# The left rows of four batches as one pair of tiles in the seven-product scheme

## The chip, the cores and the metric

The kernel runs on one core of one Trainium2 chip. The metric is the device time of one execution in microseconds (us). Five engines matter: PE multiplies matrices, DVE (VectorE) and ACT (ScalarE) do elementwise work, SP issues most transfers, and 16 DMA engines carry them. Each engine works through its own queue in order and waits at its head for semaphores. Matrix products land in PSUM, of which this kernel uses four banks for output sums (tag `acc`), two for the hidden layer (tag `h`) and two for other products (`bg`).

## The reference

```python
def _attn_ref(q, k, v, phi):                     # 8 batches, 8 heads, 576 rows, width 64, 32 memories
    a = softmax(phi over its rows)
    k_m = np.einsum('bhsm,bhsd->bhmd', a, k)
    v_m = np.einsum('bhsm,bhsd->bhmd', a, v)
    attn = softmax(scale * q @ k_m.T)
    return attn @ v_m

x = attn_out as 4608 x 512
h = x @ w_in                                     # 512 x 2048
g = h * sigmoid(h)
return g @ w_out                                 # 2048 x 512
```

## The kernel before

A batch has 576 rows: 512 main rows, which are four tiles of 128, and 64 left rows. Two batches' left rows make one tile of 128, kept in `gleft` (128 partitions, 16 chunks of the hidden width, 2 x 64 rows). Operands of the products are split into a high and a low part in a 32-bit format that PE takes at full rate, and each product is three matmuls: high x high, high x low, low x high.

Per batch, attention is folded into the first layer: `p_mm` multiplies the batch's memory with `w_in` (its result, split in two by ACT L647 and DVE L649, is the tile `pm`), and the hidden layer is attention weights (`aparts`) times `pm`. `s_back` turns the weights of the next batch into place (two transposes on DVE, L461, into a tile `aT`; a copy on ACT, L462) and `s_low` makes their low part (DVE L467).

Batches 0 and 1 work in 16 steps: `ffn1` (12 matmuls, 288 columns), `silu` (ACT L694, L696), `split`, and `ffn2` into four `acc` tiles, one per main row tile (12 matmuls of 512 columns). At the end of a batch `store` copies the four `acc` tiles on ACT (L724) and sends them out. The tiles of the first two copies share one buffer (`cva`), which the fourth copy takes again, so it waits until the first two have been sent.

Batches 2 to 7 use a scheme of seven products for a pair of row tiles and a pair of chunks, in place of eight. A batch has two pairs of tiles (t = 0, 1) and eight pairs of chunks (j): 16 steps. In each, `ffn1s` makes the hidden layer of the step (12 matmuls into `h`, one buffer), `forms` applies silu (ACT L825 into the buffer `gbuf`, L827 for the left rows), builds sums and differences (DVE L830, L833, L834), and splits them (ACT L829, L839; DVE L840, L841) into two alternating sets of buffers in `aparts` and `gparts`. `st_step` then does 7 x 3 = 21 matmuls of 256 columns into four `sum` banks. After j = 7 `st_out` copies banks 0 and 1 (ACT L884), adds (DVE L891, four adds, and three later in `rest`) and stores. PE runs `ffn1s` of step s + 1 ahead of `st_step` of step s.

Behind batches 1, 3, 5 and 7 comes a left phase of four steps for the one tile of left rows of two batches. Behind batch 1 it is plain: `left_step`, 48 matmuls of 512 columns into `accleft`, with `t1_load` fetching changed weight blocks into `wo_hi` and `wo_lo` after each step. Behind the others `left_st` does 96 matmuls of 256 columns (eight products' worth, three banks `lsum`). The operands are made by `left_split` (ACT L916, DVE L917). The left phase is also where `s_back` and `s_low` for the next even batch run (slot `NFC + 3`), with `aT` in `gbuf`, which the left phase does not use otherwise.

What sets the order: the code is written step by step; the table of events (`ev(batch, slot, function)`) says what else runs in which slot (`run`). PE and ACT follow the written order, DVE and SP are placed by a scheduler within the constraints. All transfers named `L88` go through SP's one queue in the order of issue.

## Time and profile before

| what | value |
|---|---|
| median of 3 runs | 692.94 us (692.68 to 693.82) |
| profiled execution, first to last instruction | 692.1 us |
| DVE busy | 515.7 us (75%) |
| ACT busy | 367.7 us (53%) |
| transfers | 93.93 MB, 136 GB/s mean |
| left phase behind batch 1 | from about 194.5 us |
| left phase behind batch 3, 5, 7 | from about 358.6, 521.9, 677.1 us |

A row of a timeline or of the chain gives the start in us, the duration in us, the engine, the line and operation, out<-in with shapes, a count where equal rows are merged, and in brackets the idle time before it with what ended it. A row of windows gives, per stretch, busy time and count of each engine, the granted clock of PE as a share of full speed, the share of DMA engines busy, and GB/s.

### The profile page before, as it was taken

How to read it: one execution, taken by the hardware profiler on the slowest of the kernel's cores; microseconds unless marked ns; L12 is line 12 of the kernel's file. 1: busy time of each engine (PE TensorE's matmuls, PEld its weight loads, DVE VectorE, ACT ScalarE, POOL GpSimd, SP SyncE). 2: the span in 40 equal slices, each digit the busy share in tenths (PEclk: the TensorE clock that was granted, in tenths of full speed). 3: DMA queues.
4: the chain of work that ended last, by engine and by line, in shares of the span. 5: the costliest groups of instructions: out<-in, count | busy, mean ns of one | idle time of the engine just before them, and what ended most of it. 6: DMA issues, size and time to landing. Idle time of an engine off the chain costs nothing.

```text
span 692.1 us, 14815 instructions
## 1 busy us (share of the span) xinstructions
PE 674.7 (97%) x5932; PEld 596.3 (86%) x5932; DVE 515.7 (75%) x1084; ACT 367.7 (53%) x676; POOL 0.7 (0%) x6
## 2 busy tenths in 40 slices
PE   8999999999999999999999999999999999999997
PEld 3578777887788988899998999898989989889997
DVE  3897899788938678877875668786875667776753
ACT  3788684532624545654644545564554645654441
POOL 0000000000000000000000000000000000000000
PEclk9999999999999999999999999999999999999999
DMA  9898983234261463243430335224422203210001
GB/s 342 311 336 282 310 322 129 121 108 152 76 232 25 131 212 114 77 148 123 177 117 16 117 131 166 106 93 153 172 85 79 77 2 131 90 71 17 31 1 46
DMA packets 38228, 93.93 MB, mean 136 GB/s; under 512 B 4752, under 2 KB 22032, under 8 KB 34576
## 3 DMA queue, kind: packets, MB, share of 16 engines
q1 hardware_dynamic: 37136, 90.22, 37.7%
q10 hardware_dynamic: 1024, 2.77, 1.0%
q8 instruction: 47, 0.77, 0.5%
q14 instruction: 21, 0.17, 0.1%
HBM read 77.22 MB, written 15.73 MB: 134 GB/s over the span
## 4 chain that ended last, share of the span: by engine, by line
PE 76%; DVE 6%; ACT 2%; issue 1%; DMA 1%; SPq 0%; DVEq 0%; ACTq 0%
PE sum L850 32%; PE h L811 20%; PE acc L710 7%; PE lsum L850 5%; PE h L669 4%; PE bg L631 4%; PE accleft L710 2%; PE bg L333 1%; ACT gbuf L825 1%; PE bg L380 1%; DMA fm<-fm 1%; DVE pm L649 1%; DVE gbuf L830 0%; DVE sc L428 0%; DVE smx L424 0%
## 5 line engine op out<-in xcount | busy, mean ns | idle before, releaser
L811 PE MATMUL h<-aparts,pm 128*128 128x288 f32 x1152 | 168.8, 295 | 0.1
L811 PEld LDWEIGHTS h<-aparts,pm 128*128 128x128 f32 x1152 | 157.0, 188 | 0.7 <-ACT gleft L827 0.4
L825 ACT ACTIVATE gbuf<-h 128x512 f32<-128x512 f32 x96 | 57.2, 596 | 128.7 <-PE h L811 126.7
L850 PE MATMUL sum<-wo_hi,aparts 128*128 128x256 f32 x384 | 103.9, 293 | 0.0
L830 DVE TENSOR_TENSOR gbuf<-gbuf 128x256 f32<-128x256 f32 x96 | 40.6, 423 | 81.8 <-ACT gbuf L825 81.1
L850 PE MATMUL sum<-kept,aparts 128*128 128x256 f32 x576 | 100.1, 282 | 0.0
L850 PE MATMUL sum<-wo_lo,aparts 128*128 128x256 f32 x384 | 100.0, 282 | 0.0
L850 PEld LDWEIGHTS sum<-wo_hi,aparts 128*128 128x128 f32 x384 | 72.7, 189 | 20.6 <-ACT gleft L827 16.7
L839 ACT ACTIVATE aparts<-gbuf 128x512 fp32r<-128x512 f32 x86 | 54.4, 633 | 64.0 <-DVE gbuf L834 64.0
L710 PE MATMUL acc<-wo_hi,gparts 128*128 128x512 f32 x256 | 86.3, 396 | 0.2
L850 PEld LDWEIGHTS sum<-kept,aparts 128*128 128x128 f32 x576 | 82.5, 191 | 0.0
L841 DVE TENSOR_TENSOR gparts<-gbuf,aparts 128x512 fp32r<-128x512 f32 x86 | 59.6, 693 | 18.8 <-ACT aparts L839 18.4
L850 PE MATMUL sum<-wo_hi,gparts 128*128 128x256 f32 x384 | 73.2, 281 | 0.0
L850 PEld LDWEIGHTS sum<-wo_lo,aparts 128*128 128x128 f32 x384 | 73.1, 190 | 0.0
L850 PE MATMUL sum<-kept,gparts 128*128 128x256 f32 x288 | 65.5, 282 | 0.0
L710 PEld LDWEIGHTS acc<-wo_hi,gparts 128*128 128x128 f32 x256 | 47.8, 188 | 14.5 <-issue 2.6
L850 PEld LDWEIGHTS sum<-wo_hi,gparts 128*128 128x128 f32 x384 | 59.4, 190 | 0.0
L669 PEld LDWEIGHTS h<-aparts,pm 128*128 128x128 f32 x372 | 51.8, 188 | 7.7 <-issue 2.7
L669 PE MATMUL h<-aparts,pm 128*128 128x288 f32 x372 | 56.2, 299 | 1.3 <-DVE aparts L467 1.0
L710 PE MATMUL acc<-wo_lo,gparts 128*128 128x512 f32 x128 | 50.4, 394 | 0.8 <-DVE wo_lo L182 0.7
L829 ACT ACTIVATE aparts<-gbuf 128x384 fp32r<-128x384 f32 x96 | 50.4, 525 | 0.0
L850 PEld LDWEIGHTS sum<-kept,gparts 128*128 128x128 f32 x288 | 47.9, 190 | 0.0
(206 smaller groups left out, 989.9 us busy)
## 6 DMA issues: line engine op xcount, KB each, us to landing
win<-win_saved SPq DMA_DIRECT2D x24, 1024.0 KB, 4.9
kv<-in_kv SPq DMA_DIRECT2D x28, 516.0 KB, 4.8
q<-in_q SPq DMA_DIRECT2D x16, 576.0 KB, 4.9
raw<-in_w_in SPq DMA_DIRECT2D x14, 512.0 KB, 7.5
raw<-in_w_out SPq DMA_DIRECT2D x6, 1024.0 KB, 5.8
win_saved<-win SPq DMA_DIRECT2D x4, 1024.0 KB, 8.8
phi<-in_phi SPq DMA_DIRECT2D x7, 576.0 KB, 6.3
out<-oo SPq DMA_DIRECT2D x26, 128.0 KB, 1.8
```

The source lines that it names most:

```text
L333: nc.tensor.matmul(pt[p][M * r : M * (r + 1), :KVW], e[:, p, c, M * r : M * (r + 1)], kvt[c][:, p, r], start=c == 0, stop=False, skip_grou ...
L380: nc.tensor.matmul(to[M * r : M * (r + 1)], kvT[D * p : D * (p + 1), 0, r], at[b]["q", hf][D * p : D * (p + 1), r, f : f + n], start=True, ...
L631: nc.tensor.matmul(bg[M * r : M * (r + 1), p, :w].rearrange("p (k f) -> p k f", f=P), kvT[D * p : D * (p + 1), 1, r], src[D * p : D * (p + ...
L669: nc.tensor.matmul(h[:, hf, :HALF], wt[:, p, fs], a[:, p, hf * HALF : (hf + 1) * HALF], start=n[hf] == 0, stop=n[hf] == 5, skip_group_chec ...
L710: nc.tensor.matmul(acc[key], gt[:, cs], wt[:, fc], start=fc == 0 and n == 0, stop=fc == NFC - 1 and n == 2)
L811: nc.tensor.matmul(h[:, i, :HALF], wt[:, p, f : f + P], a[:, p], start=n == 0, stop=n == 5)
L825: nc.scalar.activation(gbuf[:, :MAIN].rearrange("p (i f) -> p i f", i=2), h[:, :, :w], AF.Silu)
L829: nc.scalar.activation(hi[:, :3], g[:, 1:4], AF.Copy)
L830: nc.vector.tensor_tensor(g[:, 4:6], g[:, :1].broadcast_to([P, 2, P]), g[:, 1:3], op=ALU.subtract)
L839: nc.scalar.activation(hi[:, 3:], g[:, 4:], AF.Copy)
L841: last_split.append(nc.vector.tensor_tensor(lo[:, 3:], g[:, 4:], hi[:, 3:], op=ALU.subtract))
L850: nc.tensor.matmul(sums[bank][:, place * Q : (place + 1) * Q], gt[:, k], wt, start=bank not in begun, stop=True, skip_group_check=True,)
```

## The change

The left rows of batches 0 to 3 become one pair of tiles (t = `LEFTS`) of the seven-product scheme behind batch 3, and those of batches 4 to 7 behind batch 7. There is no left phase behind batches 1 and 5 any more. The activations of the first two batches of each four are saved to DRAM (`left_save`, 1 MB in four pieces) and fetched back, 128 KB a step, into two buffers that are the unused ends of `aparts` (`left_load`). `left_forms` builds the operands of a step from the fetched tile and `gleft`: three activations on ACT, four subtractions and three splits on DVE. A left phase has eight steps of 21 matmuls. `t1_load` moves from the left phase into the slots of batch 1. `s_back` and `s_low` always run in slot 14; for even batches `aT` is still in `gbuf`. The last matmuls of batch 1 are run behind `ffn1s` of batch 2's first step, ahead of that step's `forms`. Rows of a pair of left tiles lie in two pieces of 64 in the output, so each store is two transfers.

```diff
-    def left_step(b, n, gs):
...
+    LEFTS, WITH_LEFTS = 2, (3, 7)
...
-    def t1_load(n):
-        for j in (2 * n, 2 * n + 1):
-            for w, q in ((wo_hi, 0), (wo_lo, Q)):
-                load(as_f32(w[:, 2 * j, Q:]), saved[j][:, q : q + Q])
+    def t1_load(j):
+        for w, q in ((wo_hi, 0), (wo_lo, Q)):
+            load(as_f32(w[:, 2 * j, Q:]), saved[j][:, q : q + Q])
...
+        if t == LEFTS:
+            one, two = ([(c * S + MAIN, LEFT) for c in (a, a + 1)] for a in (b - 1, b - 3))
+        else:
+            r = b * S + 2 * t * P
+            one, two = [(r + P, P)], [(r, P)]
...
-        ev(*((b, 9) if t == 0 else (b, NFC + 1) if b % 2 else (b + 1, 3)), rest)
-
-    def left_split(b, n):
...
-    def left_st(b, n, gs):
...
+        if t == LEFTS and b == B - 1:
+            rest()
+        else:
+            ev(*((b, 9) if t == 0 else (b, NFC + 1) if t == 1 and b in WITH_LEFTS else (b + 1, 3)), rest)
+
+    left_saved = hbm.tile([P, NFC, 2 * LEFT], F32, name="left_saved")
+    left_home = [aparts[:, k, 1, TF:] for k in range(2)]
+    left_in = {}
+
+    def left_save(fcs):
+        load(left_saved[:, fcs], gleft[:, fcs])
+
+    def left_load(j):
+        load(as_f32(left_home[j % 2]), left_saved[:, 2 * j : 2 * j + 2].rearrange("p i f -> p (i f)"))
+        left_in[j] = as_f32(left_home[j % 2]).rearrange("p (i f) -> p i f", f=P)
+
+    def left_forms(j):
+
+        g = form_src
+        hi, lo = form_high[j % 2], form_low[j % 2]
+        two, one = left_in.pop(j), gleft[:, 2 * j : 2 * j + 2]
+        nc.scalar.activation(hi[:, 0:3:2], one, AF.Copy)
+        nc.scalar.activation(hi[:, 1], two[:, 1], AF.Copy)
+        nc.vector.tensor_tensor(g[:, 5], two[:, 0], two[:, 1], op=ALU.subtract)
+        nc.vector.tensor_tensor(g[:, 6], one[:, 0], g[:, 5], op=ALU.subtract)
+        nc.vector.tensor_tensor(g[:, 4], two[:, 0], one[:, 0], op=ALU.subtract)
+        s4 = nc.vector.tensor_tensor(g[:, 7], one[:, 1], g[:, 6], op=ALU.subtract)
+        nc.scalar.activation(hi[:, 3:], g[:, 4:], AF.Copy)
+        behind(nc.vector.tensor_tensor(lo[:, 0:3:2], one, hi[:, 0:3:2], op=ALU.subtract).ins, s4)
+        behind(nc.vector.tensor_tensor(lo[:, 1], two[:, 1], hi[:, 1], op=ALU.subtract).ins, s4)
+        last_split.append(nc.vector.tensor_tensor(lo[:, 3:], g[:, 4:], hi[:, 3:], op=ALU.subtract))
+        return hi, lo
...
-        turn = NFC + 3 if b % 2 else 14
+        turn = 14
...
+    for k in range(3):
+        ev(5, 10 + 2 * k, left_save, slice(4 * k, 4 * k + 4))
+    ev(6, 0, left_save, slice(12, NFC))
+    for b in WITH_LEFTS:
+        for j in range(NP):
+            ev(b, 15 if j < 2 else NFC + j - 1, left_load, j)
...
+                ev(*((b, max(2 * j + 2, int(1.5 * j + 3.5))) if j < NP - 1 else (b + 1, 0)), t1_load, j)
+            for k in range(3):
+                ev(b, 4 * k + 4, left_save, slice(4 * k, 4 * k + 4))
+            ev(b + 1, 0, left_save, slice(12, NFC))
...
             h = ffn1s(b, t, j)
+            if prev[0] == "main":
+                finish(range(NI))
+                prev = None
             part = forms(b, t, j, h)
...
-        if b % 2:
-            for n in range(NLS):
-                gs = left_split(b, n)
-                if b > 1:
-                    run(b, NFC + n)
-                finish((0, 1, 2, 3))
-                prev = ("left", b, n, gs)
+        if b in WITH_LEFTS:
+            for j in range(NP):
+                part = left_forms(j)
+                run(b, NFC + j)
+                finish(range(NI))
+                prev = ("st", b, LEFTS, j, part)
```

First place, the end of batch 1. This is PE before, from the last matmuls of the last main tile (`acc3`):

```order
L710 MATMUL acc3_1248<-wo_hi_76,gparts_79 128x512
L710 MATMUL acc3_1248<-wo_lo_77,gparts_79 128x512
L710 MATMUL acc3_1248<-wo_hi_76,gparts_79 128x512
L710 MATMUL accleft_1984<-wo_hi_76,gparts_79 128x512
L710 MATMUL accleft_1984<-wo_lo_77,gparts_79 128x512
L710 MATMUL accleft_1984<-wo_hi_76,gparts_79 128x512 x2
```

And PE after, from the same matmuls, which now stand behind the first `ffn1s` of batch 2; `h_2025` is the second `ffn1s` of batch 2, and `bg` is a `p_mm`:

```order
L709 MATMUL acc3_1249<-wo_hi_76,gparts_79 128x512
L709 MATMUL acc3_1249<-wo_lo_77,gparts_79 128x512
L709 MATMUL acc3_1249<-wo_hi_76,gparts_79 128x512
L803 MATMUL h_2025<-aparts_81,pm_1835 128x288 x12
L630 MATMUL bg_2047<-win2_2_1824,kvT2_1661 32x512 x8
L842 MATMUL sum0_2065<-wo_hi_76,aparts_81 128x256
```

ACT after, at the same place: the four stores of batch 1 (L723), and behind them the silu of batch 2's first step (L817 reads `h_1975`, L819 its left rows); this order is as before:

```order
L723 ACTIVATE oo_1991<-acc0_1237 128x512
L723 ACTIVATE oo_1991<-acc1_1241 128x512
L723 ACTIVATE o_2002<-acc2_1245 128x512
L723 ACTIVATE oo_2008<-acc3_1249 128x512
L817 ACTIVATE gbuf_82<-h_1975 128x512
L819 ACTIVATE gleft_80<-h_1975 128x2x32
```

Between the last `acc3` matmul and the second `ffn1s`, PE had the 48 matmuls of `accleft` and now has nothing; the second `ffn1s` needs the `h` buffer that L819 reads last.

Second place, ACT at the end of batch 3. Before, from the silu of its last step (`h_3850`); L916 is `left_split`, L884 the copies of banks 0 and 1, L462 the copy of `s_back`:

```order
L825 ACTIVATE gbuf_82<-h_3850 128x512
L827 ACTIVATE gleft_80<-h_3850 128x2x32
L829 ACTIVATE aparts_81<-gbuf_82 128x384
L839 ACTIVATE aparts_81<-gbuf_82 128x512
L916 ACTIVATE aparts_81<-gleft_80 128x512
L884 ACTIVATE oo_3916<-sum0_3556 128x512
L884 ACTIVATE oo_3916<-sum1_3557 128x512
L916 ACTIVATE gparts_79<-gleft_80 128x512 x2
L916 ACTIVATE aparts_81<-gleft_80 128x512
L462 ACTIVATE aparts_81<-gbuf_82 128x2x288
```

And after, where L461 is the copy of `s_back`, L817 to L831 the last step of the batch, L931, L932 and L937 the activations of `left_forms`, and L876 the copies of banks 0 and 1:

```order
L461 ACTIVATE aparts_81<-gbuf_82 128x2x288
L817 ACTIVATE gbuf_82<-h_3799 128x512
L819 ACTIVATE gleft_80<-h_3799 128x2x32
L821 ACTIVATE aparts_81<-gbuf_82 128x384
L831 ACTIVATE aparts_81<-gbuf_82 128x512
L931 ACTIVATE aparts_81<-gleft_80 128x2x128
L932 ACTIVATE aparts_81<-aparts_81 128x128
L937 ACTIVATE aparts_81<-gbuf_82 128x512
L876 ACTIVATE oo_3875<-sum0_3501 128x512
L876 ACTIVATE oo_3875<-sum1_3502 128x512
```

The copy of `s_back` has moved from behind the copies of the banks to ahead of the batch's last silu, and ahead of the copies of the banks stands L937, which waits for DVE's four subtractions.

Third place, DVE at the same time after the change, from the first step of `left_forms` (L933 to L940 are its lines; L894 is an add of `st_out`):

```order
L936 TENSOR_TENSOR gbuf_82<-gleft_80,gbuf_82 128x128
L938 TENSOR_TENSOR gparts_79<-gleft_80,aparts_81 128x2x128
L939 TENSOR_TENSOR gparts_79<-aparts_81 128x128
L940 TENSOR_TENSOR gparts_79<-gbuf_82,aparts_81 128x512
L894 TENSOR_TENSOR x_3876<-sum2_3503,oo_3875 128x256
L933 TENSOR_TENSOR gbuf_82<-aparts_81 128x128
L894 TENSOR_TENSOR x_3876<-sum2_3503,x_3876 128x256
L894 TENSOR_TENSOR oo_3875<-oo_3875 128x256
L934 TENSOR_TENSOR gbuf_82<-gleft_80,gbuf_82 128x128
L894 TENSOR_TENSOR oo_3875<-x_3876,sum3_3504 128x256
```

And before, from the only split that stood ahead of the adds (L917 is `left_split`, L891 an add of `st_out`):

```order
L917 TENSOR_TENSOR aparts_81<-gleft_80,aparts_81 128x512
L891 TENSOR_TENSOR x_3917<-sum2_3558,oo_3916 128x256
L891 TENSOR_TENSOR x_3917<-sum2_3558,x_3917 128x256
L891 TENSOR_TENSOR oo_3916<-oo_3916 128x256
L917 TENSOR_TENSOR gparts_79<-gleft_80,gparts_79 128x512
L891 TENSOR_TENSOR oo_3916<-x_3917,sum3_3559 128x256
```

The four adds that empty banks 2 and 3 now stand behind seven operations of `left_forms`, not one split, and two more of them stand between the adds. In the program after, the first step of the left pair takes the banks as they come free: its first product waits for the copy of bank 0, its third for the copy of bank 1, its fourth for the second add, its sixth for the fourth add.

More of the change, by code (lines that the diff above doesn't have):

```diff
@@ L33 @@
 NI = MAIN // P
-NLS = 4
 FULLC = S // P
@@ L734, in main_step @@
                 store((b, i), [(b * S + i * P, P)])
-    def left_step(b, n, gs):
-        for i in range(NI):
-            ffn2(gs, slice(i * P, (i + 1) * P), n * NI + i, (b, "left"))
-        if n == NLS - 1:
-            store((b, "left"), [((b - 1) * S + MAIN, LEFT), (b * S + MAIN, LEFT)], b == B - 1)
     Q = DMODEL // 2
@@ L886, in st_out, with put @@
         c12, c22 = x[:, 0], x[:, 1]
-        r = b * S + 2 * t * P
-        one, two = slice(r + P, r + 2 * P), slice(r, r + P)
+        if t == LEFTS:
[3 more added lines that the diff above has]
+            one, two = [(r + P, P)], [(r, P)]
+        def put(rows, cs, x):
+            at_ = 0
+            for k, (r, n) in enumerate(rows):
+                (nc.scalar if k and b == B - 1 else nc.sync).dma_start(out[r : r + n, cs], x[at_ : at_ + n])
+                at_ += n
+        left, right = slice(0, Q), slice(Q, DMODEL)
         def add(to, a, c, op=ALU.add):
@@ L896, in st_out @@
         add(c21, c22, sums[3][:, :Q], ALU.subtract)
-        nc.sync.dma_start(out[one, :Q], c11)
-        nc.sync.dma_start(out[two, :Q], c21)
+        put(one, left, c11)
+        put(two, left, c21)
         def rest():
@@ L903, in rest @@
             add(c12, c12, p3)
-            nc.sync.dma_start(out[two, Q:], c22)
-            nc.sync.dma_start(out[one, Q:], c12)
-        ev(*((b, 9) if t == 0 else (b, NFC + 1) if b % 2 else (b + 1, 3)), rest)
-    def left_split(b, n):
-        flat = gparts.rearrange("p k n f -> p (k n f)")
-        home = (aparts[:, 0, 1], flat, flat[:, 2 * MAIN :], aparts[:, 1, 1])[n]
-        g = gleft[:, n * NI : (n + 1) * NI].rearrange("p c f -> p (c f)")
-        gs = home[:, :MAIN], home[:, MAIN : 2 * MAIN]
-        if b == 1:
-            return split(g, gs=gs if n == 3 else None)
-        nc.scalar.activation(gs[0], g, AF.Copy)
-        last_split.append(nc.vector.tensor_tensor(gs[1], g, gs[0], op=ALU.subtract))
-        return gs
@@ L920, in left_st @@
-    def left_st(b, n, gs):
-        if n == 0:
-            sums[:] = [ps.tile([P, DMODEL], F32, tag="acc", name=f"lsum{i}", bufs=NI) for i in range(3)]
-            begun.clear()
-        part = [x.rearrange("p (n f) -> p n f", f=P) for x in gs]
-        last = n == NLS - 1
-        if last:
-            o = sb.tile([P, DMODEL], F32, tag="cva", name="ol", bufs=1)
-            x = sb.tile([P, Q], F32, tag="cva1", name="xl", bufs=1)
-        for bank, (ks, q) in enumerate((((0,), 0), ((1,), 0), ((0, 1), 1))):
-            cs = slice(q * Q, (q + 1) * Q)
-            for i in range(2):
-                for k in ks:
-                    fc = 2 * (2 * n + i) + k
-                    product(bank, 0, part, 2 * i + k, (wo_hi[:, fc, cs], wo_lo[:, fc, cs]), HIGH + LOW)
-            if not last:
-                continue
-            if bank == 0:
-                nc.scalar.activation(x, sums[0][:, :Q], AF.Copy)
-                continue
-            nc.vector.tensor_tensor(o[:, cs], sums[bank][:, :Q], x, op=ALU.add)
-            for k, r in enumerate((b - 1, b)):
-                queue = nc.scalar if b == B - 1 and k else nc.sync
-                queue.dma_start(out[r * S + MAIN : r * S + S, cs], o[k * LEFT : (k + 1) * LEFT, cs])
@@ new lines, in rest @@
+            put(two, right, c22)
+            put(one, right, c12)
+        if t == LEFTS and b == B - 1:
[10 more added lines that the diff above has]
+        left_in[j] = as_f32(left_home[j % 2]).rearrange("p (i f) -> p i f", f=P)
@@ L1178, in finish @@
             main_step(prev[1], prev[2], prev[3], tiles)
-        elif prev[0] == "left" and tiles[0] == 0:
-            if prev[1] < 2:
-                left_step(prev[1], prev[2], prev[3])
-                t1_load(prev[2])
-            else:
-                left_st(prev[1], prev[2], prev[3])
         elif prev[0] == "st" and tiles[0] == 0:
```

## The prediction

> **What bounds the kernel now.** I read the busy shares first, then the waits of PE, then the chain of work that ended last, and last the timelines at the places that the change touches.
>
> ```profile
> PE 674.7 (97%) x5932; PEld 596.3 (86%) x5932; DVE 515.7 (75%) x1084; ACT 367.7 (53%) x676; POOL 0.7 (0%) x6
> PE 76%; DVE 6%; ACT 2%; issue 1%; DMA 1%; SPq 0%; DVEq 0%; ACTq 0%
> PE h L380 <- ACT gleft L827: 4.7, 5, 1.3
> ```
>
> PE works for 674.7 of the span's 692.1 us, the chain runs mostly over PE, and PE's dearest wait is 4.7 us in five pieces of at most 1.3. So PE is the bound: a matmul less is worth its time, and any new hole in PE costs its length. DVE (75%) and ACT have slack on the average, not at each place.
>
> **1. Work taken off PE: 5.3 us.** The chain, one row per run of matmuls (start, duration, count):
>
> ```profile
> 194.47 8.17 PE accleft L710 x36
> 204.23 2.76 PE accleft L710 x12
> 326.58 2.49 PE sum L850 x21
> 677.08 11.52 PE lsum L850 x96
> ```
>
> Batch 1's left phase is 8.17 + 2.76 = 10.93. Behind batch 7 96 matmuls take 11.52, or 0.120 each; the phases behind 3 and 5 have the same 96, and I count them alike. Together 10.93 + 3 x 11.52 = 45.5 before. After, 16 steps of 21 matmuls of the same width: 16 x 2.49 to 16 x 2.52 (21 x 0.120), 39.8 to 40.3. The saving is 5.2 to 5.7; I take 5.3.
>
> **2. A hole between batches 1 and 2: +3.3.** (Rows: chain, ACT, the transfers of 180 to 212 us with count, KB each and median us to landing, and a window with PE, PEld, DVE, ACT and POOL, the clock, the DMA share, GB/s.)
>
> ```profile
> 189.01 5.46 PE acc L710 x24
> 202.64 1.59 PE h L811 x12
> 192.53 1.22 ACT L724 ACTIVATE oo<-acc 128x512 f32<-128x512 f32 x2 [2.71 <-PE acc L710]
> 196.05 0.60 ACT L724 ACTIVATE oo<-acc 128x512 f32<-128x512 f32 x1 [1.62 <-DMA out<-oo]
> 204.26 0.60 ACT L825 ACTIVATE gbuf<-h 128x512 f32<-128x512 f32 x1 [7.61 <-PE h L811]
> 204.76 0.22 ACT L827 ACTIVATE gleft<-h 128x64 f32<-128x64 f32 x1
> out<-oo SPq DMA_DIRECT2D x3, 256.0 KB, 2.2
> 190.00:192.00 2.00, 2.00 (x10) 1.68 (x9) 2.00 (x5) 0.00 (x0) 0.00 (x0) 1.00 0.79 270
> ```
>
> Before, the fourth store copy waits on ACT until the first two are out: the second ends at 193.75, the fourth starts at 196.05, 2.30 later. PE has 8.17 us of `accleft` meanwhile. After, PE runs step 14 of batch 1 (half of 5.46, to 191.74), the first `ffn1s` of batch 2 (1.59, to 193.33), step 15 (2.73, to 196.06), and then wants the second `ffn1s`. Its `h` buffer is read by the silu, and that stands on ACT behind the four stores. Step 15 completes a tile each 0.68 us, at 194.0, 194.7, 195.4 and 196.1; the second copy ends some 0.6 behind its tile, at 195.35; the fourth copy starts 2.30 later, at 197.65. Then 0.50 to the silu's start, 0.50 to the left silu (204.26 to 204.76), 0.22 for it and 0.04 to hand over: 198.9 against 196.06, a hole of **2.85**. Behind the waiting copy stand also batch 2's splits, which come later still but inside what PE then has to do. On SP's queue 768 KB more fall here (the last weight blocks of `t1_load`, the last save, the first left loads); at 270 GB/s that is 2.9 us, part of it ahead of a store, so the hole lies between 1.3 (if no store is waited for: the fourth copy at its tile's end, 196.1, and then the same 0.50 + 0.50 + 0.26) and 2.85 + 1.65 = 4.5. I take 3.3, near the computed end.
>
> **3. `s_back` ahead of batch 3's last silu: +1.2.**
>
> ```profile
> 351.95 1.23 DVE L649 TENSOR_TENSOR pm<-bg,pm 128x1024 fp32r<-128x1024 f32 x1 [0.22 <-ACT pm L647]
> 363.02 0.83 DVE L461 STREAM_TRANSPOSE gbuf<-sc 128x288 f32<-128x288 f32 x2
> 364.61 0.76 DVE L467 TENSOR_TENSOR aparts<-gbuf,aparts 128x576 fp32r<-128x576 f32 x1 [0.75 <-ACT aparts L462]
> 353.64 0.60 ACT L825 ACTIVATE gbuf<-h 128x512 f32<-128x512 f32 x1 [1.72 <-PE h L811]
> 354.27 0.53 ACT L829 ACTIVATE aparts<-gbuf 128x384 fp32r<-128x384 f32 x1
> 355.38 0.63 ACT L839 ACTIVATE aparts<-gbuf 128x512 fp32r<-128x512 f32 x1 [0.59 <-DVE gbuf L834]
> 355.96 0.28 PE L850 MATMUL sum<-wo_hi,aparts 128*128 128x256 f32 x1
> ```
>
> `s_back` and `s_low` take 363.02 to 365.37, 2.35 us, and hold `gbuf`, which the silu needs. In slot 14 they start behind L649 (353.18 less an overlap of 0.09) and free `gbuf` at 353.09 + 2.35 = 355.44, so the silu starts at 355.48, not 353.64: 1.84 late. Its first high parts are ready at 354.80 + 1.84 = 356.64, and PE wants them at 355.96: 0.68. Six matmuls later (0.72) it wants the parts of L839, ready at 356.01 + 1.84 = 357.85, and stands at 357.36: 0.5 more. Together 1.2. Behind batch 5 there is no L649 ahead of it in that slot; the same reckoning leaves +0.3. If DVE gets to the transposes early, both are nothing.
>
> **4. The banks' hand-over at a left phase: +1.2 behind batch 7, +1.9 behind batch 3.**
>
> ```profile
> 673.17 0.29 DVE L833 TENSOR_TENSOR gbuf<-gbuf 128x128 f32<-128x128 f32 x1
> 673.50 0.29 DVE L834 TENSOR_TENSOR gbuf<-gbuf 128x128 f32<-128x128 f32 x1
> 673.71 0.55 DVE L840 TENSOR_TENSOR gparts<-gbuf,aparts 128x384 fp32r<-128x384 f32 x1
> 674.49 0.69 DVE L841 TENSOR_TENSOR gparts<-gbuf,aparts 128x512 fp32r<-128x512 f32 x1 [0.23 <-ACT aparts L839]
> 675.10 0.69 DVE L917 TENSOR_TENSOR aparts<-gleft,aparts 128x512 fp32r<-128x512 f32 x1
> 676.04 0.60 ACT L884 ACTIVATE oo<-sum 128x512 f32<-128x512 f32 x1 [1.06 <-PE sum L850]
> 676.88 0.60 ACT L884 ACTIVATE oo<-sum 128x512 f32<-128x512 f32 x1 [0.24 <-PE sum L850]
> 676.92 0.28 PE L850 MATMUL lsum<-wo_hi,aparts 128*128 128x256 f32 x1
> 677.17 0.42 DVE L891 TENSOR_TENSOR x<-sum,oo 128x256 f32<-128x256 f32 x1 [1.39 <-ACT oo L884]
> ```
>
> An operation of this size starts 0.33 behind one it depends on and 0.21 behind one it doesn't (673.17, 673.50, 673.71). After, DVE begins the four subtractions at 675.10, L936 ends at 676.14, L937 runs from 676.18 to 676.81, and the copy of bank 0, behind it on ACT, starts at 676.72 in place of 676.04, to 677.32. PE's first product starts at 677.36, not 676.92: 0.44. DVE's splits and the first adds follow, with L933 and L934 of the next step between them; the second add ends at 678.43, and the fourth product waits for it 0.38; the fourth add ends at 679.32, and the sixth product waits 0.41. Sum 1.2. Behind batch 3 the 1.84 of part 3 comes on DVE too: 1.07 in place of 0.44, sum 1.9.
>
> **5. The end: +2.3.**
>
> ```profile
> 688.31 0.28 PE L850 MATMUL lsum<-wo_hi,aparts 128*128 128x256 f32 x1
> 688.63 0.42 DVE L940 TENSOR_TENSOR ol<-lsum,xl 128x256 f32<-128x256 f32 x1 [0.95 <-PE lsum L850]
> 679.24 1.09 DVE L891 TENSOR_TENSOR x<-x,oo 128x256 f32<-128x256 f32 x3
> ```
>
> Before, one add follows the last matmul and ends 0.74 behind its start. After, all seven adds follow: the first 0.37 behind it, then 0.46, 0.34, 0.34, 0.34, 0.34, 0.46 from start to start and 0.42 for the last: 3.07 (three in a row take 1.09 above). The last transfers are as small as before. +2.3.
>
> **6. The steps in a left phase: nothing.** ACT and DVE make a step's operands in turn: L933 to L936 1.04, L937 0.63, L940 0.69 with small gaps, 2.47, beside PE's 2.51. That is hidden by 0.04. The fetch of 128 KB is issued a step and a half ahead (3.5 us):
>
> ```profile
> wo_hi<-forms SPq DMA_DIRECT2D x8, 128.0 KB, 2.7
> ```
>
> One of that size lands in 2.7, so it is hidden as long as nothing big is ahead of it. If either cover goes, PE is short by that much in each of up to 16 steps.
>
> The saves, and `t1_load` moved into batch 1, add transfers where SP's queue has room and no compute waits; I count nothing.
>
> **Sum.** -5.3 + 3.3 + 1.2 + 0.3 + 1.9 + 1.2 + 2.3 = +4.9. The profiled span, 692.1, is 0.84 under the median, so I add the sum to the median: 692.94 + 4.9 = **697.8**. The bounds of parts 2, 3 and 4 (together about 1.5 either way) make its own range 696.3 to 699.3.
>
> **The rivals.**
>
> *The clock falls in the hole of part 2.* At the start PE had pauses, and the clock fell:
>
> ```profile
> 8.00:9.00 1.00, 0.43 (x2) 0.39 (x3) 0.51 (x3) 0.83 (x2) 0.00 (x0) 0.88 1.00 409
> 9.00:10.00 1.00, 1.00 (x4) 0.15 (x2) 0.71 (x2) 0.02 (x1) 0.00 (x0) 0.50 1.02 373
> 12.00:13.00 1.00, 1.00 (x40) 0.78 (x39) 0.00 (x0) 0.00 (x0) 0.00 (x0) 0.92 1.03 415
> ```
>
> From 8.9 to about 12.2 it was at 0.50, some 3.4 us, in which PE did half its work: a loss of 1.7. If a hole of 3 us is enough, the time is 697.8 + 1.7 = 699.5. For it: at 8 us PE was 43% busy and not idle, and the clock fell nonetheless. Against: no later pause, of 1.3 at most, lowered it. 0.20. The Trainium skill, "TensorE: Matmul & The Clock Gate", section "What's actually happening", says that the clock falls to half behind one idle window of about 3.4 us and returns behind as long a busy one. By that rule a hole of 2.85 would leave the clock alone and one of 4.5 would not.
>
> *The stores don't hold ACT up* (the other side, one mechanism). Parts 2 and the larger parts of 3 and 4 rest on ACT standing at a waiting copy while PE has run out. Parts 1 and 5 and the hand-over behind batch 7 stay: -5.3 + 2.3 + 1.2 = -1.8. If the stores land before the fourth copy wants its buffer, and DVE does the transposes early enough, part 3 and the hand-over behind batch 3 fall away, and of part 2 there remains something between nothing and its lower end, 1.3: -1.8 to -0.5, or 691.1 to 692.4. It decides from the point where the holes of PE before the end sum to less than 3.0, the saving less the tail. Against it: the wait of 1.62 on the transfer stands in the row of 196.05. 0.17, about half of it faster by more than 0.2% and half within.
>
> *DVE binds the left phases*: the margin is 0.04 a step; if it is short by 0.2, 16 x 0.2 = 3.2 more, 701. 0.05.
>
> *The holes are half as large*: 3.3 + 1.2 + 1.9 + 1.2 = 7.6 becomes 3.8, some 694.5. 0.05, slower.
>
> *The change does not save what it says*, as the products at 256 columns cost more where weights alternate: part 1 nothing, about 703. 0.03. The rows of 21 in 2.49 speak against it.
>
> **Chances and range.** Forecast 0.50, clock 0.20, no hold-up 0.17, DVE 0.05, half 0.05, no saving 0.03. 0.2% is 1.4 us, about what a measurement of this kernel tells from no change: 691.55 and 694.33. Faster 0.09, same 0.08, slower 0.83. The range leaves out the other side and the dearest case: 694.0 to 701.2.
>
> **What would show it.** Right: a row of PE with about 2.9 to 3.3 of idle time at the second `ffn1s` of batch 2, ended by ACT's left silu; the fourth store copy with a wait on a transfer ahead of it; 16 runs of 21 matmuls at 2.5; the banks' copies about 0.7 later in batch 7's last step; about 3.1 us from the last matmul's start to the end of the last add. Wrong: PE idle under 1 us at 196, or a granted clock of half behind it, or gaps inside the left steps that end on DVE's L940 or on a left load.

## The result, and the profile after

| | us | against the kernel before on the same chip |
|---|---|---|
| before | 692.81 median of 4 (692.65 to 693.82) | 1 |
| changed | 702.13 median of 4 (701.82 to 703.62) | 1.0140 (95% interval 1.0128 to 1.0152) |
| forecast | 697.8, range 694.0 to 701.2 | 1.007 |

The change makes the kernel 9.3 us slower. I had forecast slower by 4.9, and the time lies above the range. The profile below is of the execution of 703.62, the slowest of the four; its span is 9.4 us longer than the profiled span before.

The page of the changed kernel, its busy shares, and PE's three dearest waits (total, times, longest):

```profile
PE 673.4 (96%) x5932; PEld 593.9 (85%) x5932; DVE 541.8 (77%) x1184; ACT 379.8 (54%) x712; POOL 0.7 (0%) x6
...
PE h L379 <- ACT gleft L819: 4.5, 5, 1.0
PE h L803 <- ACT gleft L819: 4.3, 2, 3.2
PE sum L842 <- ACT oo L876: 1.4, 2, 0.9
```

PE was busy for 674.7 us before and is now busy for 673.4: 1.3 less, where 5.3 were to come off. Two new waits stand in the list. To see where the time goes I compared the start of the same silu on ACT (L825 before, L817 after) in both traces, step for step. The difference jumps at six places and ends within 0.2 of where it stood between them:

| same step in both | before | after | difference |
|---|---|---|---|
| last step of batch 1 (L694, L693) | 189.11 | 189.65 | +0.54 |
| batch 2, eleventh silu | 253.72 | 247.97 | -5.75 |
| batch 3, last but one | 348.32 | 342.56 | -5.76 |
| batch 4, second | 374.55 | 380.71 | +6.16 |
| batch 5, last but one | 511.60 | 517.62 | +6.02 |
| batch 6, second | 537.83 | 533.86 | -3.97 |
| batch 7, last | 672.08 | 668.12 | -3.96 |
| last matmul | 688.31 | 694.37 | +6.06 |
| end of the span | 692.1 | 701.5 | +9.4 |

Taking from each jump the matmuls that come or go there (10.93 us of the old left phase behind batch 1, 11.69 behind 3, 11.68 behind 5, 11.52 behind 7; a new left phase is 8 x 2.51 = 20.08) leaves what each place costs. Behind batch 1, for one: -5.75 - 0.54 + 10.93 = 4.6.

| term of the sum | predicted | measured |
|---|---|---|
| 1. work of PE | -5.3 | 40.16 - 45.82 = -5.7 |
| 2. batch 1 to 2 | +3.3 | +4.6 |
| 3 and 4. behind batch 3 | 1.2 + 1.9 = +3.1 | +3.5 |
| 3. behind batch 5 | +0.3 | +1.7 |
| 4. behind batch 7 | +1.2 | +1.5 |
| 5. the end | +2.3 | 7.13 - 3.79 = +3.3 |
| start and drift | 0 | +0.54 - 0.14 = +0.4 |
| sum | +4.9 (as rounded there) | +9.3 (9.4 unrounded) |

So no term had the wrong sign, and none of the costs was put too high. The rows behind them. First the end of batch 1, PE, ACT, and the windows of 1 us with PE's granted clock (the third number from the end):

```profile
196.25 0.39 PE L709 MATMUL acc<-wo_hi,gparts 128*128 128x512 f32 x1
199.85 2.66 PE L803 MATMUL h<-aparts,pm 128*128 128x288 f32 x12 [3.22 <-ACT gleft L819]
...
198.60 0.60 ACT L723 ACTIVATE oo<-acc 128x512 f32<-128x512 f32 x1 [2.01 <-DMA out<-oo]
...
200.00:201.00 1.00, 1.00 (x7) 1.00 (x8) 0.93 (x4) 0.41 (x2) 0.00 (x0) 0.79 0.70 262
201.00:202.00 1.00, 1.00 (x6) 1.00 (x5) 0.77 (x2) 0.46 (x1) 0.00 (x0) 0.50 0.00 0
202.00:203.00 1.00, 1.00 (x11) 0.39 (x17) 0.18 (x1) 0.45 (x1) 0.00 (x0) 0.50 0.00 0
203.00:204.00 1.00, 1.00 (x16) 0.00 (x0) 0.75 (x3) 0.71 (x3) 0.00 (x0) 0.51 0.00 0
```

PE stands for 3.22 us, and behind it the clock is at half: `ffn1s` takes 2.66 in place of 1.75. The four windows lose 0.21 + 0.50 + 0.50 + 0.49 = 1.7 us. The hole and one of the rivals came together: 3.2 + 1.7 = 4.9, of which 0.3 comes back inside batch 2 (PE's longest wait for the left silu at L379, 1.3 before, is 1.0).

Behind batch 3, and behind batch 5 with the DVE and ACT rows ahead of the wait:

```profile
350.99 0.39 PE L842 MATMUL sum<-wo_hi,aparts 128*128 128x256 f32 x1 [0.51 <-ACT aparts L821]
352.21 0.39 PE L842 MATMUL sum<-wo_hi,aparts 128*128 128x256 f32 x1 [0.24 <-ACT aparts L831]
355.20 0.39 PE L842 MATMUL sum<-wo_hi,aparts 128*128 128x256 f32 x1 [0.94 <-ACT oo L876]
...
526.67 1.85 PE L803 MATMUL h<-aparts,pm 128*128 128x288 f32 x12 [1.05 <-ACT gleft L819]
...
519.24 0.29 DVE L300 COPY wide<-fm 128x256 f32<-128x256 f32 x1 [0.90 <-DMA fm<-fm]
522.33 1.22 DVE L648 TENSOR_TENSOR pm<-bg,pm 128x1024 fp32r<-128x1024 f32 x1 [0.22 <-ACT pm L646]
523.48 0.83 DVE L460 STREAM_TRANSPOSE gbuf<-sc 128x288 f32<-128x288 f32 x2
...
525.91 0.60 ACT L817 ACTIVATE gbuf<-h 128x512 f32<-128x512 f32 x1 [0.89 <-DVE aparts L466]
```

Both places are one picture: L648, then the transposes, then the silu, late by 1.9 behind batch 3 (-3.85 in the difference of its starts, against -5.76) and by 3.0 behind batch 5 (+8.99 against +6.02). Behind batch 5 something else comes in: in the step ahead DVE stood 0.90 us for a 1 KB transfer (`fm`), 0.36 at the same place before, and PE's wait at the second `ffn1s` of batch 6 follows that. Over the nine profiles of changed kernels, here and below, in which the buffer is still shared, PE's wait there is 0.30 where DVE doesn't stand for `fm`, 0.70 at 0.57, 1.05 at 0.90, 1.32 at 1.18 and 1.55 at 1.43.

The left steps on DVE, and the end of the program:

```profile
680.63 0.29 DVE L933 TENSOR_TENSOR gbuf<-aparts 128x128 f32<-128x128 f32 x1
682.44 0.69 DVE L940 TENSOR_TENSOR gparts<-gbuf,aparts 128x512 fp32r<-128x512 f32 x1 [0.24 <-ACT aparts L937]
683.16 0.29 DVE L933 TENSOR_TENSOR gbuf<-aparts 128x128 f32<-128x128 f32 x1
...
694.25 0.40 PE L842 MATMUL sum<-kept,gparts 128*128 128x256 f32 x2
696.54 0.76 DVE L894 TENSOR_TENSOR x<-x,oo 128x256 f32<-128x256 f32 x2
697.24 1.37 SPq L888 DMA_DIRECT2D out<-x  x2
697.51 1.26 ACTq L888 DMA_DIRECT2D out<-x  x2
```

A left step is 2.53 us on DVE (680.63 to 683.16), and at L940 DVE waits 0.24 for ACT in it. The last add ends at 697.30, 2.93 behind the last matmul's start (694.37), and then 4.2 us pass to the span's end, where before 3.05 passed.

### The profile page after: what moved, and what is told of

The parts are those of the page before. It is cut to its first block, busy times and chain, and to the rows that moved or that the text cites. A ratio compares the mean times of both kernels' runs of the same rounds, so it can differ in the third digit from the quotient of the medians.

```text
span 701.5 us, 15059 instructions
## 1 busy us (share of the span) xinstructions
PE 673.4 (96%) x5932; PEld 593.9 (85%) x5932; DVE 541.8 (77%) x1184; ACT 379.8 (54%) x712; POOL 0.7 (0%) x6
## 4 chain that ended last, share of the span: by engine, by line
PE 69%; DVE 9%; ACT 4%; DMA 2%; issue 2%; SPq 1%; DVEq 0%; ACTq 0%
PE sum L842 34%; PE h L803 18%; PE acc L709 7%; PE h L668 3%; PE bg L630 3%; PE bg L332 1%; ACT gbuf L817 1%; DVE pm L648 1%; DMA qz<-qm 1%; DVE gbuf L822 1%; PE bg L379 1%; ACT pm L646 1%; SPq L87 1%; DMA fm<-fm 1%; DVE gbuf L826 1%
## 5 line engine op out<-in xcount | busy, mean ns | idle before, releaser
L842 PE MATMUL sum<-wo_hi,aparts 128*128 128x256 f32 x448 | 121.3, 293 | 2.3 <-ACT oo L876 1.4
L817 ACT ACTIVATE gbuf<-h 128x512 f32<-128x512 f32 x96 | 57.3, 597 | 111.7 <-PE h L803 107.2
L842 PE MATMUL sum<-kept,aparts 128*128 128x256 f32 x672 | 116.9, 282 | 0.2
L842 PE MATMUL sum<-wo_lo,aparts 128*128 128x256 f32 x448 | 116.6, 282 | 0.0
L842 PEld LDWEIGHTS sum<-wo_hi,aparts 128*128 128x128 f32 x448 | 84.8, 189 | 26.5 <-ACT gleft L819 16.7
L842 PEld LDWEIGHTS sum<-kept,aparts 128*128 128x128 f32 x672 | 96.2, 191 | 0.7 <-DVE oo L894 0.7
L831 ACT ACTIVATE aparts<-gbuf 128x512 fp32r<-128x512 f32 x86 | 54.4, 633 | 64.1 <-DVE gbuf L826 64.1
L842 PE MATMUL sum<-wo_hi,gparts 128*128 128x256 f32 x448 | 85.4, 281 | 0.0
L842 PEld LDWEIGHTS sum<-wo_lo,aparts 128*128 128x128 f32 x448 | 85.2, 190 | 0.0
L842 PE MATMUL sum<-kept,gparts 128*128 128x256 f32 x336 | 76.4, 282 | 0.0
L842 PEld LDWEIGHTS sum<-wo_hi,gparts 128*128 128x128 f32 x448 | 69.3, 190 | 0.0
L842 PEld LDWEIGHTS sum<-kept,gparts 128*128 128x128 f32 x336 | 55.9, 190 | 0.0
```

What stands on the lines that cost most here:

```text
L817: nc.scalar.activation(gbuf[:, :MAIN].rearrange("p (i f) -> p i f", i=2), h[:, :, :w], AF.Silu)
L831: nc.scalar.activation(hi[:, 3:], g[:, 4:], AF.Copy)
L842: nc.tensor.matmul(sums[bank][:, place * Q : (place + 1) * Q], gt[:, k], wt, start=bank not in begun, stop=True, skip_group_check=True,)
```

## The experiments

All ratios are to the kernel before, run on the same chip in the same job.

| run | us (median) | ratio and 95% interval |
|---|---|---|
| the changed kernel again | 701.06 | 1.0121 (1.0107 to 1.0135) |
| idle matmuls in the hole | 699.57 | 1.0095 (1.0079 to 1.0112) |
| fourth store, own buffer | 698.30 | 1.0080 (1.0063 to 1.0096) |
| and the silus ahead of the stores | 696.89 | 1.0063 (1.0051 to 1.0076) |
| s_back, own buffer | 699.69 | 1.0099 (1.0074 to 1.0124) |
| early add at the end | 700.97 | 1.0114 (1.0095 to 1.0132) |
| hand-over rearranged | 702.31 | 1.0136 (1.0120 to 1.0151) |
| halves of gbuf by turns | 700.89 | 1.0114 (1.0100 to 1.0128) |
| L933 twice | 705.03 | 1.0175 (1.0161 to 1.0189) |
| three edits | 694.74 | 1.0031 (1.0019 to 1.0042) |
| six edits | 693.57 | 1.0014 (1.0005 to 1.0023) |
| before, with s_back moved alone | 695.69 | 1.0042 (1.0029 to 1.0056) |

**The changed kernel again**, as the control.

> The changed kernel once more, unaltered, on the chip of the next three runs. Theory (the hole of about 3 us between batches 1 and 2 lies at the edge of what takes the clock down, so that one execution loses 1.7 us and another nothing): a ratio to before between 1.011 and 1.015, and times that spread over 2 us. Rival (the clock falls in every execution): 1.014 and times within 0.5 us.

Its ratio is the theory's, its four times lie within 0.3 us as the rival had it. In the profile PE's hole is 2.95 us and the clock falls behind it. The spread came in other runs, below.

**Idle matmuls in the hole.**

```diff
                 finish(range(NI))
+                keep_warm(bgtile()[:, 0], 12)
                 prev = None
```

> The changed kernel with 12 idle matmuls (bf16, 512 columns, into a bank that nobody reads) on PE between the last matmuls of batch 1 and the second ffn1s of batch 2, inside the hole of 3.2 us. Theory (the clock falls behind the hole, four us at about half, and costs 1.4 us on top of the wait): the wait for ACT's left silu stays, as the idle matmuls only fill it, the granted clock stays at 1.00 behind it, and the time falls by 1.3 to 1.6 us, to about 700.7 from 702.1. Rival (the whole 4.6 us is the wait and what stands behind it on ACT): the time stays at 702.1, or rises by what the idle matmuls overrun.

```profile
194.41 2.76 PE L79 MATMUL bg<-ident 128*128 128x512 bf16 x12
197.51 1.85 PE L803 MATMUL h<-aparts,pm 128*128 128x288 f32 x12 [0.34 <-ACT gleft L819]
```

The wait for the left silu is where it was; only PE isn't idle. Up to the last matmul the clock stays at full, and the time falls by 1.5 against the control's median (1.8 by the ratios, as the two ran on different chips; 2.6 against the first run of the change). That is the clock's part of the term, without the wait's.

Does a hole of this length take the clock down each time? The control, and the run with the halves of gbuf by turns (below), which changes nothing at this place (PE's row, then the window behind it):

```profile
197.61 2.91 PE L803 MATMUL h<-aparts,pm 128*128 128x288 f32 x12 [2.95 <-ACT gleft L819]
198.00:200.00 2.00, 2.00 (x11) 2.00 (x10) 1.68 (x4) 0.63 (x1) 0.00 (x0) 0.51 0.26 95
```

```profile
197.73 1.86 PE L803 MATMUL h<-aparts,pm 128*128 128x288 f32 x12 [3.16 <-ACT gleft L819]
198.00:200.00 2.00, 2.00 (x25) 1.54 (x27) 1.70 (x5) 1.13 (x3) 0.00 (x0) 1.00 0.32 121
```

No: 2.95 us of idle time took it down to half, 3.16 did not. Of the seven profiles that have this hole unfilled, the clock fell in three (2.95, 3.22, 3.25 us) and stayed in four (2.91, 2.92, 2.97, 3.16). In two of those four the profiled execution is the fastest of its run by about 1 us (699.37 beside 700.57 to 701.21, and 699.66 beside 700.69 to 701.78); in the other two it lies among the others. So what the hole costs is 3, or 3 + 1.7, by the execution.

What decides stands in the clock's own times. Where it falls more than once in a profile, the falls lie a whole number of 3.413 us apart (the last of each profile comes behind the last matmul; the times are from the trace's clock records, which are finer than the windows above): at 9.43, 200.58 and 698.92 in the changed kernel (56 and 146 times), at 197.77, 518.63 and 699.53 in the run with s_back's own buffer (94 and 53 times). So I cut each trace into windows on this grid, counted from its own fall at the end. The windows over the hole, of the changed kernel, of the control and of the run with the halves of gbuf by turns (the second number is PE's busy time):

```profile
197.16:200.58 3.42, 0.72 (x5) 0.73 (x6) 0.79 (x3) 1.64 (x4) 0.00 (x0) 1.00 0.48 183
...
194.62:198.04 3.42, 0.47 (x4) 0.44 (x4) 0.54 (x2) 1.64 (x4) 0.00 (x0) 1.00 0.55 209
...
192.54:195.95 3.41, 2.03 (x9) 1.32 (x8) 0.00 (x0) 1.79 (x3) 0.00 (x0) 1.00 0.90 321
195.95:199.37 3.42, 1.64 (x12) 1.63 (x12) 1.48 (x4) 2.27 (x5) 0.00 (x0) 1.00 0.30 112
```

In the first two most of the hole lies in one window, and the clock is at half in the next; in the third the hole is divided between two windows, and the clock stays. The other four agree: 0.40 of PE's time in the window ahead of the fall, and 1.67 to 2.25 in the windows of the three that stayed. Over all 14 profiles of this case, from 20 us on, each window with PE busy for 1.48 us or less was followed by half clock, and none with 1.59 or more was. At the start the same limit doesn't hold: 2.0 and 2.1 us were followed by a fall in the profiles of the changed kernel and of the kernel before. Where the grid lies to the program differs from execution to execution. The Trainium skill, "TensorE: Matmul & The Clock Gate", section "What's actually happening", speaks of windows of about 3.4 us that run on freely and don't begin anew with the kernel. The traces agree with that. They don't agree with the rule that the prediction cites from there, one idle window, if the window has to be idle as a whole: a hole of 2.95 us can't fill one.

**The fourth store's own buffer**, and then also **the silus ahead of the stores**.

```diff
-            if key[1] in (0, 3):
+            if key[1] == 0:
                 homes.append(sb.tile([P, 2, DMODEL], F32, tag="cva", name="oo", bufs=1))
-            o = homes[-1][:, key[1] not in (0, 3)]
+            o = sb.tile([P, DMODEL], F32, tag="y", name="o3", bufs=1) if key[1] == 3 else homes[-1][:, key[1]]
...
             h = ffn1s(b, t, j)
+            silus(b, t, j, h)
             if prev[0] == "main":
```

(`silus` is the first two activations of `forms`, which then begins with its splits.)

> The changed kernel with a buffer of its own for the fourth store copy of batch 1, so that it doesn't wait for the first two transfers. Theory (the hole of 3.2 us is the landing of the stores, 2.0 of it, and it takes the clock down): the hole shrinks to about 1.3 us, the clock stays up, the time falls by 2.0 + 1.4 = 3.4 us, to 698.7. Rival (the clock falls behind a hole of 1.3 too): 2.0 us, to 700.1. Rival (PE waits for something else at the same place, a transfer or batch 2's operands): less than 1 us.

> The changed kernel with a buffer of its own for the fourth store copy and with the two silus of batch 2's first step ahead of the four store copies on ACT. Theory (the second ffn1s waits only for ACT's place in its queue): no wait of PE at that ffn1s, clock at 1.00, 1.4 us less than with the own buffer alone, a ratio to before of about 1.006 (697.0). Rival (behind the silus the splits of that step come late, behind the stores, and PE waits for them): the hole moves to the first st_step of batch 2 and half or more of it stays, 1.007 or more.

```profile
195.95 1.85 PE L803 MATMUL h<-aparts,pm 128*128 128x288 f32 x12 [1.29 <-ACT gleft L819]
```

With its own buffer the hole is 1.29, as the lower end of part 2 had it (1.3), and the clock stays: 698.3 for 698.7 expected. The expectation counted from the first run of the change; against the control's ratio it is 2.8 us less, for 3.4. With the silus ahead the wait is gone altogether: 696.9 for 697.0 expected. The whole term, 4.2 us against the control, hung on the stores that stood ahead of the silus on ACT and on their shared buffer.

**`s_back` in a buffer of its own.**

```diff
-        if b > 2 and b % 2 == 0 and u == FIRST:
-            aT = gbuf[:, : 2 * w].rearrange("p (g s) -> p g s", g=2)
-        else:
-            aT = sb.tile([P, 2, w], F32, tag=tag, name=f"aT{b}", bufs=1)
+        aT = sb.tile([P, 2, w], F32, tag=tag, name=f"aT{b}", bufs=1)
```

> The changed kernel with s_back's transposes in a buffer of their own (the one that odd batches use), in the same slot. Theory (the silu of the last step waits for the shared buffer): behind batch 3 it starts 1.0 us earlier (ACT still has the copy of s_back ahead of it) and PE's 0.75 us of waits for the operands go, with some 0.5 of the banks' hand-over; behind batch 5 the wait of 1.1 us for the left silu goes. In all 2.3 us less, to 699.8. Rival (the place in the queues of DVE and ACT is what delays, not the buffer): the silu starts as late as before, and the time falls by less than 0.5.

The six times spread from 697.2 to 703.3, so the ratio settles little. In the profiled execution, the slowest of the six, something else happened at batch 5 (DVE, then PE):

```profile
513.02 0.20 DVE L293 TENSOR_REDUCE fm<-qz 32x8 f32<-32x32 f32 x1 [2.08 <-DMA qz<-qm]
...
517.20 1.09 PE L627 MATMUL bg<-win,kvT 64*32 64x512 f32 x16 [2.08 <-DVE pm L645]
```

DVE waited 2.08 us for a transfer of 1 KB, PE waited as long, and the clock fell behind that too (in the window of the grid ahead of it, 515.21 to 518.63, PE was busy for 1.43 us). In the change that transfer's median time to landing at batch 5 is 3.9 us, and 1.7 before; over all changed kernels it is 2.4 to 5.7, and 1.7 again in the last run below, which moves `s_back` alone. The saves of 256 KB and two fetches of 128 KB now stand around it. For the 1 KB transfers of this place, `qz` and `fm`, DVE stands 0.5 to 2.1 us in every profile of a changed kernel, and 0.36 and 0.20 us in the two kernels without saves. No run leaves out the saves alone, so that they are the cause is argued and not shown. I had counted the saves at nothing.

The run of three edits, below, shows this edit without that wait.

**The early add at the end.**

```diff
+        if t == LEFTS and b == B - 1:
+            s = sb.tile([P, Q], F32, tag="mx", name="c11", bufs=1)
+            add(s, c11, c21)
+            put(one, left, s)
+            add(c12, sums[2][:, :Q], c11)
...
```

> The changed kernel with one of the seven adds of the last st_out (c11 + c21) done before the sums of bank 2 arrive, into a buffer of its own, and its two transfers issued first. Theory (the end is one chain of six adds behind the last matmul, and then transfers that queue two deep at their issue): one add less (0.34) and the first pair of transfers out of the way of the last (0.6): 0.8 to 1.0 us less, to 701.2. Rival (only the adds count): 0.3 less, to 701.8. Rival (the landing of a small transfer alone sets the end): nothing.

From the last matmul's start to the span's end it is 6.3 us (691.21 to 697.5), 7.2 in the control (691.63 to 698.8). Of the 0.9, 0.27 is the add (the last one ends 2.66 behind the matmul, 2.93 in the control), the rest is a pair of transfers out of the queue. The medians don't show it: 700.97 is 0.1 under the control's, 0.5 by the ratios, inside the intervals. So the size rests on the two profiles. By them, what I had left out at the end is the issue of the transfers: in the changed kernel each queue issues the last two in 1.26 to 1.37 us, and the last landing waits for the second.

**The hand-over rearranged**: ACT's copies of banks 0 and 1 around L937, the three splits of the first left step behind st_out's four adds.

```diff
             nc.scalar.activation(o[:, i], sums[i], AF.Copy)
+            if i == 0 and put_off:
+                nc.scalar.activation(put_off[0][0][:, 3:], form_src[:, 4:], AF.Copy)
...
+        if j == 0:
+            put_off.append((hi, lo, two, one, s4))
+            return hi, lo
...
```

> The changed kernel with the first step of each left phase rearranged: the copies of banks 0 and 1 stand on ACT around L937 and not behind it, and DVE does the four adds of st_out ahead of the three splits. Theory (the hand-over is paid to this order): the first product starts without a wait, and of the 1.3 and 1.9 us behind batches 7 and 3 most is saved, 2.0 to 2.5 us less in all. Rival (DVE has eleven operations to do before PE can go on, in whichever order, and a wait that goes comes back at the low parts and in the next step): 0.5 us less or nothing.

My theory fell. The first product now starts without a wait, and the median is 1.2 us over the control's (the intervals overlap, 1.0120 to 1.0151 and 1.0107 to 1.0135); from the batch's last silu to the last matmul behind batch 7 it is 27.43 us (665.84 to 693.27), 26.25 in the control. In the next two steps PE stands at L945's high parts, which ACT makes late (it waited 2.99 for DVE's differences):

```profile
674.89 0.63 ACT L945 ACTIVATE aparts<-gbuf 128x512 fp32r<-128x512 f32 x1 [2.99 <-DVE gbuf L941]
...
675.57 0.38 PE L842 MATMUL sum<-wo_hi,aparts 128*128 128x256 f32 x1 [0.33 <-ACT aparts L945]
678.86 0.38 PE L842 MATMUL sum<-wo_hi,aparts 128*128 128x256 f32 x1 [0.52 <-ACT aparts L945]
```

DVE has the same operations to do, later, and nothing in the steps behind lets it catch up.

**L933 twice**, and **the two halves of gbuf by turns**, are about that.

```diff
+        nc.vector.tensor_tensor(g[:, 5], two[:, 0], two[:, 1], op=ALU.subtract)
         nc.vector.tensor_tensor(g[:, 5], two[:, 0], two[:, 1], op=ALU.subtract)
```

```diff
-        g = form_src
+        g = form_src[:, j % 2 * 4 : j % 2 * 4 + 4]
```

> The changed kernel with one of the four subtractions of left_forms (L933) done twice, in all 16 left steps: 0.20 us more on DVE in each. Theory (DVE and ACT make a step in 2.53 us beside PE's 2.51, so the cover is used up): PE has to wait from some step on, and of 16 x 0.20 = 3.2 us about 2.4 come through. Rival (the cover holds, as the steps run at PE's pace): less than 0.5 us.

> The changed kernel with the four differences of left_forms in the two halves of gbuf by turns, so that DVE need not finish L940 of one step before it begins the next. Theory (the 2.53 us of a left step are a loop through DVE, ACT and DVE, and not DVE's work, which is 2.0): DVE runs ahead after two steps, and of what the hand-over costs the part that DVE passes on goes, some 0.5 us at each left phase: a ratio to before 0.0015 under the control's 1.0121. Rival (PE waits for the banks, not for the operands): the same as the control within 0.2 us.

```profile
680.26 0.29 DVE L933 TENSOR_TENSOR gbuf<-aparts 128x128 f32<-128x128 f32 x1
...
683.11 0.29 DVE L933 TENSOR_TENSOR gbuf<-aparts 128x128 f32<-128x128 f32 x1
...
670.73 0.39 PE L842 MATMUL sum<-wo_hi,aparts 128*128 128x256 f32 x1 [0.22 <-DVE x L894]
671.73 0.74 PE L842 MATMUL sum<-kept,aparts 128*128 128x256 f32 x4 [0.26 <-DVE oo L894]
```

The last two rows are PE's, in the run with the halves by turns. With L933 twice a step is 2.85 us, 0.32 more (the second one stands in the chain of dependent operations, so it costs more than the 0.20 that I had put), and the kernel is 4.0 us slower than the control: of 16 x 0.32 = 5.1 four fifths come through. The cover that part 6 saw, 0.04, isn't there. With the halves by turns two steps take DVE 4.5 us (L933 at 679.23 and 683.75, with one between), so DVE is freed; the time stays, 700.89, and from the last silu of batch 7 to the last matmul it is 26.09 us beside 26.25. Behind batch 3 it is 0.2 less too, where the theory had 0.5 at each. The medians, of different chips, can't tell the two apart; by the traces the rival is nearer: PE waits for the banks there (DVE's adds that empty them), and freeing the operands brings little as long as the banks are late.

**Three edits, and six edits, together.**

> The changed kernel with three of the edits together: the silus ahead of the stores and the fourth store's own buffer, s_back's own buffer, and the early add of the tail. Theory (the terms are apart, each at its place): 696.9 less 0.85 at the end, 0.75 behind batch 3 and 1.1 behind batch 5, which makes 694.2, a ratio to before of 1.002; no clock drop inside the span, and the second wait for the left silu (batch 6) under 0.3 us. Rival (behind batch 5 it is the transfers of the weights' maxima, now with the saves around them in SP's queue, that delay the transposes): the wait there stays at 1 us, 695.3.

> The three edits with three more: the two halves of gbuf by turns in the left steps, the sum p5 + p3 of the last st_out made on GpSimd beside DVE, and the low products of the last step in the order of banks 1, 2, 3. Theory: 694.2 less 1.0 at the hand-overs and 0.4 at the end, 692.8, no difference from before (ratio 0.999 to 1.001): the saved 5.3 us of PE are then all given back, by 2.5 at the end, 2 at the hand-overs and the rest at the last steps of the batches. Rival (the terms overlap): 694 or more.

The three make 694.74, between the theory's 694.2 and the rival's 695.3. Beside the first run's differences of silu starts, 0.65 us come off behind batch 3 and 1.0 behind batch 5, where the wait is now 0.24 although DVE still stands 1.11 for `fm` in the step ahead. So a wait of over 0.3 there needs both, the shared buffer and the late transfer:

```profile
519.50 1.86 PE L800 MATMUL h<-aparts,pm 128*128 128x288 f32 x12 [0.24 <-ACT gleft L813]
```

The six make 693.57 where the theory had 692.8 and the rival 694 or more: neither. That is still 0.14% over before, with an interval that leaves out 1. No version here beats the kernel before. The low products' order and GpSimd's sum were worth under 0.1 (6.26 us from the last matmul's start to the end, 6.30 with three edits) and not 0.4: the last add ends 0.4 earlier behind that matmul (2.27 and 2.67), but 4.0 us of transfers follow it, and 3.6 with three edits.

**`s_back` moved in the kernel before, nothing else.**

```diff
-        turn = NFC + 3 if b % 2 else 14
+        turn = 14
```

> The kernel before with one part of the change alone: s_back and s_low of batches 3 and 5 in slot 14, with the transposes still in gbuf, and nothing else changed. Theory (the silu of the last step waits some 1.9 us for the buffer, also behind batch 5, where a p_mm split stands ahead of the transposes on DVE as it does behind batch 3): PE waits 0.75 us for that step's operands behind each of the two batches, and little more, since the old left phase takes the hand-over: 1.5 to 2.0 us more, 694.3 to 694.8. As I predicted it: 1.2 behind batch 3 and 0.3 behind batch 5, 694.2, with no wait of over 0.3 behind batch 5. Rival (the old left phase hides it): within 0.5 us of before.

```profile
355.67 0.38 PE L850 MATMUL sum<-wo_hi,aparts 128*128 128x256 f32 x1 [1.01 <-ACT aparts L829]
356.89 0.39 PE L850 MATMUL sum<-wo_hi,aparts 128*128 128x256 f32 x1 [0.24 <-ACT aparts L839]
...
520.44 0.39 PE L850 MATMUL sum<-wo_hi,aparts 128*128 128x256 f32 x1 [0.77 <-ACT aparts L829]
521.66 0.39 PE L850 MATMUL sum<-wo_hi,aparts 128*128 128x256 f32 x1 [0.24 <-ACT aparts L839]
```

2.9 us for this part alone, where I had 1.2 + 0.3 and the theory 1.5 to 2.0; the rival falls. The two batches look alike: by the silu starts it costs 1.75 us behind batch 3 and 1.5 behind batch 5, of which the waits shown are 1.25 and 1.0. Where the rest lies, 0.5 at each, isn't known. The old left phase doesn't hide it.

## Why the prediction was wrong, by its own steps

The direction held, and the waits that the sum names came where it put them. Three steps failed: the clock was taken as an alternative to part 2 and not as a piece of it, part 3 misread the rows at batch 5 and, with part 6, left out DVE's longer wait for the 1 KB transfers there, and part 5 left out the issue of the transfers. They are 1.3 + 1.4 + 1.0 = 3.7 of the 4.4 to 4.5 us that were missing; the rest (+0.4 behind batch 3, +0.3 behind batch 7, +0.4 of start and drift, -0.4 of PE's work) is small.

- **Part 1** held: -5.7 for -5.3.
- **Part 2** was 3.3 by the wait alone, and 3.22 is what the wait was, at the fourth store copy as computed. What failed is the choice between forecast and rival: the clock fell as well, for 1.7, in the profiled execution, in the control, and not in every run. I read "no later pause, of 1.3 at most, lowered it" as speaking against; it spoke only of pauses under half as long. The clock was a part of this term, not an alternative to it. The chance of 0.20 was too low for a hole that I put at 3.3 us: it fell in three profiles of seven. What decided was PE's busy time in one window of the clock's grid, and not the hole's length alone.
- **Part 3, behind batch 5**, is the one step with a wrong reading: "Behind batch 5 there is no L649 ahead of it in that slot". The trace of before has it (L649 at 515.55, ahead of the last silu at 516.92), I had looked at the left phase only. 1.7 for 0.3; alone in the kernel before the move costs 2.9 for 1.5. In the changed kernel the reading is only half of it: the 1.05 us of PE's wait there follow DVE's wait for `fm`, and 0.30 is left where DVE doesn't stand. So the 0.3 would have held for that wait, had the transfers come as before; some 0.5 more of the term is no wait that the rows show.
- **Part 4** was right to 0.3 us a place (1.5 for 1.2; 3.5 for 3.1 with part 3). Its reason was half right: PE waits for the banks; rearranging ACT's copies and DVE's adds for them doesn't help.
- **Part 5**: the adds are as computed (2.93 for 3.07 to the end of the last one). "The last transfers are as small as before" was true and beside the point: there are twice as many, and each queue has two to issue behind the last adds, not one. 1.0 more.
- **Part 6** came out by luck. 2.53 on DVE is over PE's 2.51, not under it, which adds nothing over eight steps but leaves no cover for anything. Its other half, that no compute waits for the saves, most likely failed at batch 5: DVE stands longer for the 1 KB transfers in each profile of a changed kernel (0.90 here), and in one execution PE stood 2.08 us with it.
- **The range** let one surplus happen at a time. The upper end, 701.2, lay just over the dearest rival that it kept, DVE's 701. Three of the terms were short at once, and 697.8 + 3.7 is 701.5. (The rival with holes half as large also comes to 692.94 + 4.9 - 3.8 = 694.0 and not 694.5, inside the range by a hair.)

Why do the first run of the change and the control differ (1.0140 and 1.0121; spans of 701.5 and 698.8 us in the profiles)? In the profile of the first run the clock fell once more, at the start, and in the control's it didn't (the first run, then the control):

```profile
10.00:11.00 1.00, 1.00 (x17) 0.63 (x20) 0.57 (x2) 0.67 (x2) 0.00 (x0) 0.50 1.07 370
...
10.00:11.00 1.00, 1.00 (x37) 0.74 (x33) 0.03 (x1) 0.68 (x2) 0.00 (x0) 1.00 1.11 365
```

That is 1.7 of the 2.7 us between the two profiles. The profile before has the same fall (8.75 to 12.16), so it is in none of the terms above. What stays open is why the medians differ too, as no profile of the other executions was kept; where the 0.5 us at each batch go when `s_back` is moved alone; and the 0.5 us behind batch 5 that no wait shows.

## What to carry to other kernels

Work that is taken away between two stages was also a cover; look for what it hid on every engine at that place (here ACT's store copies, the banks' adds on DVE, and a buffer that was free only there), and price each with its own rows. When a hole of PE can touch the clock, the clock's loss is added to the hole, with a chance that depends on where the hole falls on the clock's grid; it isn't a case of its own. And where several terms rest on the same optimism, let the range hold their sum.
